# Diagonal matrices made earlier, C's products woven between part A's products, carried states by one more identity product

## The chip, the cores and the metric

One core of a Trainium2 chip runs the whole program. TensorE multiplies, VectorE (DVE) and ScalarE (ACT) work element by element, GpSimd (POOL) sets small tiles, and SyncE (SP) issues nearly all transfers. The metric is the device time of one execution in microseconds (us). The kernel before took 145.25 us, the median of three runs (145.24 to 145.46).

## The reference

The output has two halves side by side, of 2048 rows and 448 columns each.

Part A is a linear recurrence with complex diagonal state (448 states) over 2048 steps:

```python
Lam_bar = jnp.exp(dt * Lam)
B_bar = ((Lam_bar - 1.0) / Lam)[:, None] * Bmat
Bu = jnp.einsum("bld,pd->blp", x + 0j, B_bar)
for t in range(L):
    h = Lam_bar[None, :] * h + Bu[:, t, :]
y = 2.0 * jnp.einsum("blp,dp->bld", hseq, Cmat).real + x * Dskip[None, None, :]
```

Part B is attention with 16 heads of 28 columns, where each position sees itself and seven earlier ones, two steps apart:

```python
qkv = (x @ wqkv).reshape(B, S, 3, H, Dh)          # q, k, v
idx = pos[:, None] - (jnp.arange(8) * 2)[None, :] # positions looked at
logits = einsum("bhsd,bhswd->bhsw", q, k[idx]) * Dh ** -0.5   # -1e9 where idx < 0
o = einsum("bhsw,bhswd->bhsd", softmax(logits), v[idx])
out = o.reshape(B, S, D) @ wo
```

## The kernel before

**Part A.** A complex state is held as a pair of real ones, so the 448 states are seven tiles (m = 0 to 6) of 128 partitions, 64 real and 64 imaginary. Multiplying the states by a power of Lam_bar is a product on TensorE with a 128x128 matrix of four diagonal blocks. `mat` (L595) makes such a matrix for all seven m at once on VectorE, out of a pattern `Dm` and the powers in `Scat`. The powers are listed in `KPOW` (L44): index 0 to 5 are the powers 1, 2, 3, 4, 8 and 12, index 6 to 12 are 16 up to 1024; one more, "g", scales C. `mats_behind` (L590) makes several of them and puts each behind a given VectorE instruction.

The 2048 steps are split into 512 groups of four. Level 1 (`level1_halves` L653 for m = 0 to 3, `level1` L632 for the rest) computes the state inside each group, h[0] to h[3], each from the one before. `scan` (L665) sums four groups to one and then doubles over 128 columns in seven rounds, each a product with a power and a cast on ScalarE. It runs three times, for m = 0 to 3, 4 to 5 and 6. `ends` (L688) builds the states at the ends of all groups, G: three of every four columns by six products, the fourth by a copy on ScalarE (L693). `correct` (L706) adds to h[b] what came into the group, M[b+1] times G, in one of two ways: "A" adds h by an identity product and casts on ScalarE (two products), "V" has one product and an add on VectorE (L715). `y` (L722) makes an output tile from four products with the skip vector's diagonal `Dg` (made in `skip`, L580) and seven with C. C is loaded as rows (`load_c`), transposed by a transfer (`turn_c`, L501) and multiplied by "g" (`setup_c`, L609).

**Part B.** q, k and v are products of x with weights. VectorE multiplies q with shifted k (`products`, L298, each in a queue behind the one before, `queued` L293), and TensorE sums over a head's columns with 0/1 matrices (`sums`, L315). `softmax(hf)` (L344) has five steps: two transposes with maxima on VectorE, two products that subtract the maxima, followed by exponentials on ScalarE, and the sums `den` with the reciprocal `rec` on VectorE. `pv` (L400) multiplies the weights with shifted v and adds up, on VectorE, for eight w; after each w it runs what its list `between` has. The last rows that a shift needs come by `halo` copies (L235). `tail` (L422) transposes the sums by a transfer into oT and multiplies by wo.

**The order.** TensorE's order is written out by hand: every product is chained behind the one before (`chain`, L85). In `lanes` (L97) products of 64 rows run in two lanes, upper and lower half of the array, one step of the loop giving one product to each lane. `weave` is a list of (step, functions): when the loop reaches the step, the functions run and their products stand between those of the lanes. These are called visits here. Behind the lanes, scans, level 1, `ends` and wo's first products follow, and then a list `line` of corrections and y products, into which the products of the "V" corrections are put at fixed distances (L871 to L877). All other engines' instructions are put in an order before the run by a planner that starts what its own costs hold to be ready, in program order where several are. PSUM has eight banks: four with tag "mm", two "pt" and two "lg"; `ps` (L75) takes a bank by tag, and an instruction that writes a bank waits until its former content has been read. The lanes use "mm" and "pt" in turn, the softmaxes "lg".

Of the kernel before, what the change touches and what calls it, by code (L numbers as in the profile page):

```python
# [14 lines left out]
f32 = mybir.dt.float32  # L15
# [3 lines left out]
D = 448  # L19
T = 16  # L20
NCH = 128
KT = 4
KP = 112
KA = 128
NF = 512
# [9 lines left out]
NM = 7  # L35
# [3 lines left out]
PAD = 64  # L39
MH = ((0, 4), (4, 6), (6, 7))  # L40
# [3 lines left out]
KPOW = [1, 2, 3, 4, 8, 12] + [T << s_ for s_ in range(NST)]  # L44
NPW = len(KPOW)
# [401 lines left out]
class PartA:  # L447
# [132 lines left out]
    def skip(self):  # L580
        nc, ident = self.nc, self.cx.ident
        ptd = self.cx.ps([KA, KT], bf16, "pt_d", "lg")
        self.cx.chain(nc.tensor.transpose(ptd[:], self.drow[:], ident[0:KT, 0:KT]).ins)
        dsk = self.pool.tile([KA, KT], f32, name="dsk")
        nc.scalar.copy(dsk[:], ptd[:])
        self.Dg = self.pool.tile([KA, KT, KA], bf16, name="Dg")
        for k in range(KT):
            nc.scalar.activation(self.Dg[:, k, :], ident[:], ACT.Copy, scale=dsk[:, k:k + 1])

    def mats_behind(self, keys, after):  # L590
        for i in keys:
            key = "g" if i == "g" else KPOW[i]
            self.cx.order(self.mat(key, self.Scat[:, NPW if i == "g" else i]), after, "NoSync")
# [12 lines left out]
            self.mats[key] = t_[:].rearrange("p h q m -> p m (h q)")  # L606
        return self.nc.vector.tensor_tensor(t_[:], in0, in1, op=ALU.mult).ins  # L607

    def setup_c(self, eng):  # L609

        for m in range(NM):
            ps = self.cx.ps([NCH, D], f32, "c_ps", "pt")
            self.nc.tensor.matmul(ps[:], lhsT=self.mats["g"][:, m, :], rhs=self.cT[:, :, m, :], start=True, stop=True)
            self.cx.ev(eng, self.C[:, m, :], ps[:])

    def alloc_h(self):
        pool = self.pool
# [70 lines left out]
    def ends(self, mh):  # L688
        nc, cx = self.nc, self.cx
        M, v = self.mats, self.h[3]  # L690
        hc = self.pbuf[mh][NST % 2]
        gv = self.G[:, :, 1:1 + NF].rearrange("p m (c a) -> p m c a", a=4)
        nc.scalar.copy(gv[:, MH[mh][0]:MH[mh][1], :, 3], hc[:, :, PAD:PAD + NCH])  # L693
        for m in range(*MH[mh]):
            vm = v[:, m, :]
            hp = hc[:, m - MH[mh][0], PAD - 1:PAD - 1 + NCH]
            ps = cx.ps([NCH, 3 * NCH], f32, "gt", "mm")
            mm = [(cx.ident[:], vm[:, 0:3 * NCH], 0, 3), (M[4][:, m, :], vm[:, 0:2 * NCH], 1, 3),
                  (M[8][:, m, :], vm[:, 0:NCH], 2, 3), (M[4][:, m, :], hp, 0, 1), (M[8][:, m, :], hp, 1, 2),
                  (M[12][:, m, :], hp, 2, 3)]  # L700
            for i, (l_, r_, c0, c1) in enumerate(mm):
                nc.tensor.matmul(ps[:, c0 * NCH:c1 * NCH], lhsT=l_, rhs=r_, start=(i == 0), stop=(i == 5),  # L702
                                 skip_group_check=True)
            nc.scalar.copy(gv[:, m, :, 0:3], ps[:].rearrange("p (a c) -> p c a", a=3))

    def correct(self, b, m, eng):  # L706
        nc, cx, out = self.nc, self.cx, []
# [31 lines left out]
@with_exitstack  # L739
def body(ctx: ExitStack, tc: tile.TileContext, A_x, A_Lre, A_Lim, A_Bre, A_Bim, A_Cre, A_Cim, A_logdt, A_Dskip,  # L740
         B_x, B_wqkv, B_wo, out):
    nc = tc.nc
    pool = ctx.enter_context(tc.tile_pool(name="sb", bufs=1))
    psum = ctx.enter_context(tc.tile_pool(name="ps", bufs=1, space=bass.MemoryType.PSUM))
    out_v = out[0].rearrange("(p j) e -> p j e", j=T)
    cx = Ctx(tc, pool, psum)
    b = PartB(cx, B_x, B_wqkv, B_wo, out_v[:, :, D:2 * D])
    a = PartA(cx, A_x, A_Lre, A_Lim, A_Bre, A_Bim, A_Cre, A_Cim, A_logdt, A_Dskip, out[0].rearrange("(n b) e -> n b e", b=4)[:, :, 0:D])
    parts = ((512, 1024), (1024, 1536), (1536, 2048))
    b.alloc()  # L750
    b.load_xn(0, 2)
    a.load_params()
    b.load_w(D, 0, D, nc.scalar)
    b.load_xn(2, 4)
    cx.consts()
    a.consts()
    b.clear()
    nc.scalar.activation(cx.spot2[:], cx.wz[0:1, 0:1], ACT.Exp)
    b.load_w(0, D, D, nc.sync)
    for g in parts:  # L760
        b.load_x(*g)
    b.consts()
    b.load_w(2 * D, 2 * D, D, nc.sync)
    a.load_bc()
    a.load_d()
    a.load_x()
    a.turn_b()
    b.zero_halo(b.vd)
    b.load_wo()
    a.load_c()  # L770
    cx.warm(8)
    a.turn_params()
    turns = [lambda i=i: b.turn_x(i, "VAVV"[i], ("pt", "lg")[i // 2]) for i in range(4)]
    for f in turns[:2]:
        for ins in f():
            cx.chain(ins)
    a.params(b.turned["V"])
    cx.warm(2)

    def later():  # L780
        b.mix_w(a.reduced)
        return ()

    def first():
        b.products(0, 0)
        return ()

    def second():
        b.products(0, 0, (2,), (2,))
        return ()  # L790

    def third():
        b.products(0, 1, (0, 1))
        return ()

    values = [b.proj(j, "A") for j in (*range(HJ, T), 6, 7, 4, 5, 2, 3, 0, 1)]
    qk, soft = b.qk(), {}
    weave = [(5, turns[2:] + [later]), (BEGIN[0], [first]), (BEGIN[1], [second]), (BEGIN[2], [third])]
    weave += [(s_, [f]) for s_, f in zip(WEAVE, qk)]
    weave.sort(key=lambda x: x[0])  # L800

    def turn():
        a.mats_behind(["g"], b.product)
        soft[1] = b.softmax(1)
        return soft[1][0][0]() + soft[1][0][1]()

    def prepare():
        a.mats_behind([0, 3, 4], b.maxima)
        return soft[1][0][4]()

    def begin():
        b.halo(b.vd, 6, HALO)
        b.halo(b.vd, 0, 6)
        a.turn_c()
        a.skip()
        a.alloc_h()
        soft[0] = fs, at0 = b.softmax(0)

        def put(*fs):
            return lambda after: [x for f in fs for x in ((f() if callable(f) else a.mats_behind([f], after)) or ())]  # L820

        soft["pv"] = b.pv(1, soft[1][1], 0, 4, between=[put(*fs[:2]), put(5, 6), put(*fs[2:4]), put(7, 8), put(fs[4]), put(9, 10)])
        soft["put"] = put
        return more()

    def more():
        return next(soft["pv"]) + next(soft["pv"])

    weave += [(168, [turn])] + [(171 + 2 * i, [lambda i=i: soft[1][0][2 + i]()]) for i in range(2)] + [(177, [prepare])]
    weave += [(181, [begin]), (205, [more]), (215, [more])]  # L830
    cx.lanes([b.proj_t(t0, t1, g, "A") for t0, t1, gs in ((0, 256, (0, 1, 2, 4, 5, 6)), (256, 512, (0, 1, 2)), (0, 512, (3,)), (256, 512, (4, 5, 6)))
              for g in gs]
             + [b.proj_t(*t, g, "A") for t in parts for g in range(7)] + values
             + [a.level1_halves(b_, m) for b_ in range(4) for m in range(*MH[0])], weave, 20)
    at0, put, wo = soft[0][1], soft["put"], b.outs
    deque(soft["pv"], 0)
    deque(b.pv(1, soft[1][1], 4, 8, between=[put(11, 12), put(), put(1, 2)]), 0)
    a.alloc_scan()
    for mh in range(3):
        if mh:  # L840
            a.level1(mh)
        a.scan(mh)
        if mh == 0:
            a.setup_c("A")
    cx.order(wo[0]()[0][0], a.last, "NoSync")
    for mh in range(3):
        a.ends(mh)
    cx.ya = pool.tile([NCH, 8, D], bf16, name="ya", tag="cn")
    line, extra, steps = [], [], []
    todo = [(b_, m) for b_ in (1, 2) for m in range(NM)][2:]  # L850

    def each(ins):
        cx.vchain(ins)
        steps.append(ins)
        if len(steps) >= 7 and todo:
            extra.extend(a.correct(*todo.pop(0), "V"))

    def wo_line(lists):
        return [(i, 0.19) for l_ in lists for i in l_]

    for b_, m in [(0, m) for m in range(NM)] + [(1, 0), (1, 1)]:
        line += a.correct(b_, m, "A")
    line += wo_line(wo[1]())
    deque(b.pv(0, at0, 0, 4, each=each), 0)
    deque(b.pv(0, at0, 4, 8, True, each=each), 0)
    for b_, r in itertools.product((3, 0, 1, 2), range(4)):
        line += a.y(r, b_)
        if (b_, r) == (1, 3):
            line += wo_line(wo[2]())
    line += wo_line([wo[3](i) for i in range(2)])  # L870
    t, n = 0.0, 0  # L871
    for ins, dt in line:
        if n < len(extra) and t >= 1.55 * n:
            cx.chain(extra[n][0])
            t, n = t + extra[n][1], n + 1
        cx.chain(ins)
        t += dt  # L877
# [31 lines left out]
```

## Time and profile before

| | |
|---|---|
| median of three runs | 145.25 us |
| the profiled execution | 145.12 us |
| its span, first to last instruction | 143.2 us |
| TensorE busy | 137.2 us (96%) |
| VectorE busy | 123.2 us (86%) |
| ScalarE busy | 90.9 us (63%) |
| share of the last chain on TensorE / VectorE | 69% / 23% |

The span is the part of the execution from its first to its last instruction. A row of a timeline gives start, busy time, engine, line, operation, tile written and tiles read, and, in brackets, how long the engine was idle before it and what ended the wait. For TensorE the busy time of a row includes the pipeline's end, so the distance between two starts, not the row's own length, is what a product costs. The chain that ended last goes back from the last instruction to what released each; an engine can be on it that another would have held up anyway.

### The profile page before, as it was taken

Reading aid. Unit: us, or ns where it says so; the run is one execution under the profiler, and the core shown is the slowest. Engines: PE = TensorE matmul, PEld = TensorE weight load, DVE = VectorE, ACT = ScalarE, POOL = GpSimd, SP = SyncE. Lnnn points to the kernel's source line nnn. Section 1 sums busy time; section 2 is a strip of 40 time slices with the busy share of each in tenths; the row PEclk is TensorE's granted clock in tenths of the full one; section 3 lists DMA queues with packets and bytes.
Section 4 is the critical chain, followed back from the end, with each engine's and each line's share of the span. In section 5 each row is a group of like instructions: output and inputs, shape, how many; then the busy total and the mean of one; then the engine's idle time right before and its main releaser. Section 6 shows DMA issues by size and latency. Waiting matters only on the chain.

```text
span 143.2 us, 3302 instructions
## 1 busy us (share of the span) xinstructions
PE 137.2 (96%) x1260; PEld 78.0 (54%) x1260; DVE 123.2 (86%) x153; ACT 90.9 (63%) x200; POOL 10.5 (7%) x108
## 2 busy tenths in 40 slices
PE   6999999999999998999999999999999999999991
PEld 2466445444666654446665456668556555555540
DVE  4488764989999889999999999999999999999011
ACT  3476678667786766583589897889973222435440
POOL 7211100100000000000101000000000000000000
PEclk9999999999999999999999999999999999999999
DMA  4989899899964979990003800018102182211963
GB/s 114 293 171 143 199 209 158 149 197 159 169 122 96 184 112 278 247 195 0 0 0 64 69 0 0 0 30 198 36 32 98 64 174 89 95 64 64 136 221 128
DMA packets 45166, 17.03 MB, mean 119 GB/s; under 512 B 37267, under 2 KB 44769, under 8 KB 45151
## 3 DMA queue, kind: packets, MB, share of 16 engines
q1 hardware_dynamic: 44586, 16.36, 58.1%
q10 hardware_dynamic: 565, 0.46, 1.1%
q8 instruction: 10, 0.16, 0.5%
q14 instruction: 5, 0.04, 0.1%
HBM read 3.91 MB, written 3.67 MB: 53 GB/s over the span
## 4 chain that ended last, share of the span: by engine, by line
PE 69%; DVE 23%; ACT 3%; issue 2%; POOL 0%; DVEq 0%; ACTq 0%; POOLq 0%
PE qk_ps L130 16%; PE y_ps L731 15%; DVE pvb L414 8%; PE wo_ps L437 7%; DVE pvb L417 6%; PE v_ps L130 5%; PE lg L323 5%; PE l L638 5%; PE co L711 3%; PE warm L73 3%; DVE pr L312 2%; DVE mat L607 2%; PE y_ps L727 2%; PE gt L702 2%; PE l L683 2%
## 5 line engine op out<-in xcount | busy, mean ns | idle before, releaser
L414 DVE TENSOR_TENSOR pvb<-attn,vd 128x1792 bf16<-128x1792 bf16 (+1 forms) x33 | 34.3, 1063 | 0.0
L417 DVE TENSOR_TENSOR pvb<-pvb 128x1792 bf16<-128x1792 bf16 (+1 forms) x29 | 30.8, 1061 | 0.3
L130 PE MATMUL qk_ps<-xbT,wqkv_nat 64*128 64x512 bf16 (+1 forms) x210 | 24.0, 335 | 0.4 <-POOL spot L139 0.3
L312 DVE TENSOR_TENSOR pr<-q,kd 128x3072 bf16<-128x3072 bf16 x11 | 19.0, 1754 | 3.8 <-ACT q L156 3.4
L734 ACT CAST ya<-y_ps 128x448 bf16<-128x448 f32 x16 | 8.5, 532 | 17.2 <-PE y_ps L731 16.1
L731 PE MATMUL y_ps<-Ccat,h 128*128 128x448 bf16 x84 | 17.9, 353 | 0.0
L130 PEld LDWEIGHTS <-wqkv_nat 64*128 64x128 bf16 x210 | 11.0, 94 | 10.7 <-POOL spot L139 3.1
L130 PE MATMUL l1h<-xaT,Bcat 64*128 64x512 bf16 x112 | 15.4, 377 | 0.0
L437 PE MATMUL wo_ps<-wo_p,oT 128*128 128x448 bf16 x64 | 13.9, 352 | 0.0
L638 PE MATMUL l<-xaT,Bcat 128*128 128x512 bf16 x48 | 13.6, 379 | 0.0
L156 ACT CAST kd<-qk_ps 128x512 bf16<-128x512 f32 (+4 forms) x26 | 10.4, 423 | 4.5 <-PE qk_ps L130 4.3
L130 PE MATMUL v_ps<-wqkv_nat,xbT 64*128 64x448 bf16 x112 | 13.1, 360 | 0.0
L156 ACT CAST q<-qk_ps 128x512 bf16<-128x512 f32 (+2 forms) x23 | 9.9, 456 | 2.0 <-PE qk_ps L130 1.8
L731 PEld LDWEIGHTS <-h 128*128 128x128 bf16 x84 | 7.5, 98 | 5.6
L139 POOL MEMSET spot<- 1x1 f32 x63 | 5.6, 89 | 59.5 <-PE qk_ps L130 25.6
L156 ACT CAST vd<-v_ps 128x448 bf16<-128x448 f32 x16 | 7.6, 528 | 3.7 <-PE v_ps L130 3.5
L130 PEld LDWEIGHTS <-Bcat 64*128 64x128 bf16 x112 | 7.0, 94 | 5.3 <-issue 0.4
L312 DVE TENSOR_TENSOR kd<-q,kd 128x3072 bf16<-128x3072 bf16 x5 | 8.8, 1755 | 1.2 <-ACT q L156 1.2
L686 ACT CAST pbuf<-l 128x512 bf16<-128x512 f32 (+2 forms) x21 | 8.7, 416 | 1.4 <-PE l L683 1.2
L130 PEld LDWEIGHTS <-xbT 64*128 64x128 bf16 x112 | 7.3, 145 | 4.1 <-issue 1.3
L437 PEld LDWEIGHTS <-oT 128*128 128x128 bf16 x64 | 6.0, 98 | 5.5 <-issue 0.6
L649 ACT CAST h<-l1h 128x512 bf16<-128x512 f32 x12 | 6.3, 602 | 3.5 <-PE l1h L130 3.5
(133 smaller groups left out, 218.9 us busy)
## 6 DMA issues: line engine op xcount, KB each, us to landing
out_dram<-ya SPq DMA_DIRECT2D x20, 112.0 KB, 1.7
out_dram<-yb SPq DMA_DIRECT2D x12, 112.0 KB, 3.0
vd<-vd SPq DMA_DIRECT2D x1, 784.0 KB, 5.6
wqkv_nat<-in_B_wqkv_dram SPq DMA_DIRECT2D x2, 336.0 KB
vd<-vd SPq DMA_DIRECT2D x1, 588.0 KB
xn<-in_B_x_dram SPq DMA_DIRECT2D x2, 224.0 KB, 3.8
cn<-in_A_C_re_dram SPq DMA_DIRECT2D x4, 98.0 KB, 3.1
cn<-in_A_C_im_dram SPq DMA_DIRECT2D x4, 98.0 KB, 3.2
```

The costliest lines, as they stand in the source:

```text
L130: ins = mm(g["ps"], lhsT=l_, rhs=r_, start=first, stop=not (g["left"][0] or g["left"][1]), skip_group_check=True).ins
L156: return self.nc.scalar.copy(out, in_).ins
L312: self.queued(V.tensor_tensor(pr, q[0][:, qu].unsqueeze(2).to_broadcast([KA, KT - 1, 4, n]), self.shifted(self.kT[:, 2 * i + qu], s), op=A ...
L323: out.append(mm(lg[32 * t:32 * t + 32, n * qu:n * qu + n], lhsT=l_, rhs=r_, start=not (s or qu or c), stop=(s == 1 and c == KT - 1), skip_ ...
L414: each(V.tensor_tensor(t_[:, c0:c1], at[:, w, jl0 + c0:jl0 + c1, :].unsqueeze(2).to_broadcast([NCH, c1 - c0, DH, H]), self.vd[:, off + c0: ...
L417: ins = V.tensor_tensor(acc[:, c0:c1], acc[:, c0:c1], t_[:, c0:c1], op=ALU.add).ins
L437: done.append(nc.tensor.matmul(ps[:], lhsT=oT[:, 7 * i + 3 * odd + k, :], rhs=self.wo_p[:, odd, k, :], start=(k == 0), stop=(k == KT - 1)) ...
L638: nc.tensor.matmul(ps[:], lhsT=self.Bcat[:, m, k, :], rhs=self.xT[:, b, k, :], start=(k == 0), stop=(b == 0 and k == KT - 1))
L649: self.nc.scalar.copy(h, ps)
L686: nc.scalar.copy(dst[:, :, PAD:], ps[:])
L731: out.append(nc.tensor.matmul(ps[:], lhsT=self.state(m, r, b), rhs=self.C[:, m, :], start=False, stop=(m == NM - 1), skip_group_check=True ...
L734: nc.scalar.copy(ya, ps[:])
```

## The change

Five edits, all in the order and form of the work:

- The matrices M[1], M[4], "g" and M[8] are made among the first products of q and k (`early`, queued with them). In their former places come others: three in `turn`, three in `prepare`, and the list `between` of the first pv is left without mats.
- C's seven products become visits in the lanes at steps 218, 222, 226 and 242, with banks of tag "lg" instead of "pt". `turn_c` moves ahead of the halo copies in `begin`, and the skip vector's diagonal moves from `begin` to step 242.
- The two later visits of the first pv, with the steps of softmax 0, move from steps 205 and 215 to 199 and 211.
- The fourth column of G comes from a seventh product in `ends`, with the identity, and one cast of 512 columns; the copy goes.
- Corrections: five instead of nine of kind "A", sixteen instead of twelve of kind "V", which start behind the ninth VectorE instruction of the last pv pair instead of the seventh.

```diff
     def skip(self):
...
-        self.cx.chain(nc.tensor.transpose(ptd[:], self.drow[:], ident[0:KT, 0:KT]).ins)
+        out = [nc.tensor.transpose(ptd[:], self.drow[:], ident[0:KT, 0:KT]).ins]
...
+        return out
...
-    def setup_c(self, eng):
-
-        for m in range(NM):
-            ps = self.cx.ps([NCH, D], f32, "c_ps", "pt")
-            self.nc.tensor.matmul(ps[:], lhsT=self.mats["g"][:, m, :], rhs=self.cT[:, :, m, :], start=True, stop=True)
-            self.cx.ev(eng, self.C[:, m, :], ps[:])
+    def setup_c(self, *ms):
+
+        out = []
+        for m in ms:
+            ps = self.cx.ps([NCH, D], f32, "c_ps", "lg")
+            out.append(self.nc.tensor.matmul(ps[:], lhsT=self.mats["g"][:, m, :], rhs=self.cT[:, :, m, :], start=True, stop=True).ins)
+            self.cx.ev("A", self.C[:, m, :], ps[:])
+        return out
...
-        gv = self.G[:, :, 1:1 + NF].rearrange("p m (c a) -> p m c a", a=4)
-        nc.scalar.copy(gv[:, MH[mh][0]:MH[mh][1], :, 3], hc[:, :, PAD:PAD + NCH])
...
-            ps = cx.ps([NCH, 3 * NCH], f32, "gt", "mm")
+            ps = cx.ps([NCH, NF], f32, "gt", "mm")
...
-                  (M[12][:, m, :], hp, 2, 3)]
+                  (M[12][:, m, :], hp, 2, 3), (cx.ident[:], hc[:, m - MH[mh][0], PAD:PAD + NCH], 3, 4)]
...
-            nc.scalar.copy(gv[:, m, :, 0:3], ps[:].rearrange("p (a c) -> p c a", a=3))
+            nc.scalar.copy(self.G[:, m, 1:1 + NF].rearrange("p (c a) -> p c a", a=4),
+                           ps[:].rearrange("p (a c) -> p c a", a=4))
...
+    def early(*keys):
+        for k in keys:
+            ins = a.mat("g" if k == "g" else KPOW[k], a.Scat[:, NPW if k == "g" else k])
+            if b.product is not None:
+                cx.order(ins, b.product, "NoSync")
+            b.product = ins
+
     def first():
+        early(0)
         b.products(0, 0)
         return ()
 
     def second():
         b.products(0, 0, (2,), (2,))
+        early(3)
         return ()
 
     def third():
         b.products(0, 1, (0, 1))
+        early("g", 4)
         return ()
...
     def turn():
-        a.mats_behind(["g"], b.product)
+        a.mats_behind([5, 6, 7], b.product)
...
     def prepare():
-        a.mats_behind([0, 3, 4], b.maxima)
+        a.mats_behind([8, 9, 10], b.maxima)
...
     def begin():
+        a.turn_c()
         b.halo(b.vd, 6, HALO)
         b.halo(b.vd, 0, 6)
-        a.turn_c()
-        a.skip()
         a.alloc_h()
...
-        soft["pv"] = b.pv(1, soft[1][1], 0, 4, between=[put(*fs[:2]), put(5, 6), put(*fs[2:4]), put(7, 8), put(fs[4]), put(9, 10)])
+        soft["pv"] = b.pv(1, soft[1][1], 0, 4, between=[put(*fs[:2]), put(), put(*fs[2:4]), put(), put(fs[4])])
...
-    weave += [(181, [begin]), (205, [more]), (215, [more])]
+    weave += [(181, [begin]), (199, [more]), (211, [more])]
+    weave += [(218 + 4 * m, [lambda m=m: a.setup_c(m, m + 1)]) for m in (0, 2, 4)] + [(242, [lambda: a.setup_c(6), a.skip])]
...
-        if mh == 0:
-            a.setup_c("A")
...
-    todo = [(b_, m) for b_ in (1, 2) for m in range(NM)][2:]
+    todo = [(b_, m) for b_ in range(3) for m in range(NM)][5:]
...
-        if len(steps) >= 7 and todo:
+        if len(steps) >= 9 and todo:
...
-    for b_, m in [(0, m) for m in range(NM)] + [(1, 0), (1, 1)]:
-        line += a.correct(b_, m, "A")
+    for m in range(5):
+        line += a.correct(0, m, "A")
```

More of the change, by code (lines that the diff above doesn't have):

```diff
@@ L696, in ends @@
             hp = hc[:, m - MH[mh][0], PAD - 1:PAD - 1 + NCH]
-            ps = cx.ps([NCH, 3 * NCH], f32, "gt", "mm")
+            ps = cx.ps([NCH, NF], f32, "gt", "mm")
             mm = [(cx.ident[:], vm[:, 0:3 * NCH], 0, 3), (M[4][:, m, :], vm[:, 0:2 * NCH], 1, 3),
                   (M[8][:, m, :], vm[:, 0:NCH], 2, 3), (M[4][:, m, :], hp, 0, 1), (M[8][:, m, :], hp, 1, 2),
-                  (M[12][:, m, :], hp, 2, 3)]
+                  (M[12][:, m, :], hp, 2, 3), (cx.ident[:], hc[:, m - MH[mh][0], PAD:PAD + NCH], 3, 4)]
             for i, (l_, r_, c0, c1) in enumerate(mm):
-                nc.tensor.matmul(ps[:, c0 * NCH:c1 * NCH], lhsT=l_, rhs=r_, start=(i == 0), stop=(i == 5),
+                nc.tensor.matmul(ps[:, c0 * NCH:c1 * NCH], lhsT=l_, rhs=r_, start=(i == 0), stop=(i == 6),
                                  skip_group_check=True)
-            nc.scalar.copy(gv[:, m, :, 0:3], ps[:].rearrange("p (a c) -> p c a", a=3))
+            nc.scalar.copy(self.G[:, m, 1:1 + NF].rearrange("p (c a) -> p c a", a=4),
+                           ps[:].rearrange("p (a c) -> p c a", a=4))
     def correct(self, b, m, eng):
```

## The prediction

> **What bounds the kernel now.** I read the page's busy shares first, then the chain that ended last, then the timelines of TensorE, VectorE and SyncE between 45 and 100 us. Busy shares:
>
> ```profile
> PE 137.2 (96%) x1260; PEld 78.0 (54%) x1260; DVE 123.2 (86%) x153; ACT 90.9 (63%) x200; POOL 10.5 (7%) x108
> ```
>
> TensorE is idle for 6.0 us of 143.2: 1.25 before its first product, 3.2 behind its last, 1.5 in all between. So a change pays by taking products off TensorE, and costs whatever makes TensorE wait. The chain confirms it from 99.9 us on, with TensorE alone down to the last cast:
>
> ```profile
> 1.25 3.59 PE warm L73 x8
> ...
> 100.13 0.21 PE co L710
> 100.34 0.22 PE co L711
> ...
> 140.02 0.62 DVE ya L158
> ```
>
> The first row matters below: eight products of 512 columns took 3.59 us, 0.449 each, where a 512-column product takes 0.2155 later (the spacing of the "co" rows). TensorE started from idle at half rate (the page's line of granted clock does not show it; the durations do), and the two "warm" products of 5.93 us still took 0.405 each, so that lasted till about 6.7, some 5.4 us.
>
> VectorE's timeline has three holes early on, in the column of idle time before a row:
>
> ```profile
> 11.23 3.43 DVE L312 TENSOR_TENSOR pr<-q,kd 128x3072 bf16<-128x3072 bf16 x2 [0.78 <-ACT q L156]
> 16.79 1.76 DVE L312 TENSOR_TENSOR kd<-q,kd 128x3072 bf16<-128x3072 bf16 x1 [0.83 <-ACT q L156]
> 23.30 1.76 DVE L312 TENSOR_TENSOR pr<-q,kd 128x3072 bf16<-128x3072 bf16 x1 [2.59 <-ACT q L156]
> ```
>
> The most telling pair is one product on TensorE and its reader on VectorE:
>
> ```profile
> 63.64 0.62 PE L370 MATMUL den<-e,ident 128*128 128x128 bf16 x8
> 72.79 0.96 DVE L373 RECIPROCAL rec<-den 128x128 bf16<-128x128 f32 x1
> ```
>
> The sums of the second softmax (den) are finished at 64.2, but VectorE, whose order is fixed before the run, reads them 8.6 us later, behind the add of w=6. In program order the reciprocal stands behind the add of w=5. So the planner that wrote the order did not expect den at three picks (w=6 product, w=7 product, add of w=6), which start 14.6 to 16.6 us behind the first pv product of 55.16: it takes the 64-row products to be slower than they are. From den of softmax 1 (visit at step 177) to this one (step 215) lie 38 steps of the loop at L106, real spacing 0.2155 us; to miss those picks it must reckon with about 0.45 each, both halves in a row instead of side by side. Nobody in this kernel suffers: den's bank (tag "lg", two banks) is next wanted by wo_ps, after 91 us.
>
> The transpose for C, and the skip vector's cost:
>
> ```profile
> 57.82 5.12 SPq L505 DMA_TRANSPOSE Ccat<-cn  x1
> 55.17 0.41 PE L355 MATMUL lt<-ident,lgs 128*128 128x128 bf16 x4 [0.38 <-ACT dsk L585]
> ```
>
> **The change, part by part.** Durations are of the profiled execution: 145.12 us, 143.2 of it the span; the median of the runs, 145.25, is 0.13 more.
>
> Early mats. One mat costs VectorE 0.60 us (spacing of the L607 rows), g 1.75. M[1] goes in the hole of 0.78, M[4] in that of 0.83, g and M[8], 2.35, in that of 2.59. Slack 0.18, 0.23, 0.24, so 0; behind them queue the q-k products, and if a hole shrank by its slack, the sums on TensorE would come some 0.2 later. In turn(), three mats (1.80) take g's place (1.75), in prepare() three take the place of three: 0. Six mats, 3.6 us, leave the pv sequence, four of them (2.4) ahead of the reciprocal. VectorE is not what ends the kernel: its last add ends at 132.56, TensorE's y products at 136.83.
>
> Identity products. Nine corrections with a product more become five: 4 x 0.2155 = -0.86 on TensorE. VectorE takes four adds more, 4 x 0.60 = 2.4, covered by the 3.6 that left, as is the later start of its adds (behind nine pv operations instead of seven, 2.0). Uncovered, its end would come 2.4 later; the last transpose of oT behind it landed at 137.2 and is wanted at 138.4, so 1.2 would show.
>
> Carried states. Seven identity products of 128 columns, 0.055 each (row L673): +0.38 on TensorE. ScalarE loses three copies (L693: 1.36, 0.78, 0.49) and its L704 casts grow from 384 to 512 columns, 0.50 to about 0.59 (row L686). ScalarE has room: 0.
>
> The skip vector leaves the visit at step 181. There the second half of lt waited for its bank (row above); the next step began at 55.50 and now does at about 54.75: -0.75. At step 242 it costs 0.06 and part of a visit.
>
> The visit for the exponentials moves from step 205 to 199. TensorE would be there at 58.9, but VectorE's second maximum ends at 59.45: +0.4. The denominator's visit, step 215 to 211, then runs at 62.4 to 62.95 and step 218 comes at 64.5.
>
> C's products as visits. Seven products of 0.187 move from the scan to the lanes: 0 net, since the scan's steps keep level 1's products as cover (57 of 0.2155, 12.3 us; the first scan took 10.0 from its first cast at 73.39 to its last). Each visit costs beyond its products 0.11 us (den: 0.55 for eight of 0.055), so four cost +0.44. The wait of 0.21 for a mat at 81.17 goes: -0.21.
>
> SyncE. Programmed first in begin(), the transpose now needs the C loads (landed 55.3) and the last v product (54.2); the halo copies queue behind it if it goes out first. It landed 8.4 us after issue, at 66.26. If the halos still go first, C's first product waits for that landing; if it goes first, it lands by 63.8, and the halo rows for w=5 land at about 65.8 instead of 59.0, 1.4 late for VectorE.
>
> The wait for den's bank. C's first two products at step 218 take both "lg" banks, and one is den's, free only when the reciprocal has read it. VectorE's order decides. Without the mats, from 55.16: two products, maximum, add, maximum bring it to 59.37, then one pv operation per 1.0 us. The planner expected den between 16.6 and 17.6 us into the sequence (the last pick that missed it and the one that took it); four steps of 0.45 and some 0.3 for the skip vector less, that is 14.5 to 15.5. VectorE's picks now lie at 14.2, 15.2 and 16.2, so the reciprocal follows eleven pv operations, or one more or less: it starts at 70.4 (69.4 to 71.4) and ends at 71.35. TensorE runs in order and stands from 64.5, but for one short product, to 71.35. Before, step 218 came at 64.84: +6.51. The bounds for this wait are 0 (reciprocal done by 64.5) and 9.3 (reciprocal unmoved at 72.79, done 73.75).
>
> The clock behind the wait. No row shows TensorE idle for over 0.4 us after the start. Bounds: 0, as with those short gaps, and 2.7, half of those 5.4 us. The nearest row for a start from several idle us is the first: the eight products lost 3.59 - 8 x 0.2155 = 1.87, and I take that. [...]
>
> Sum: +6.51, then -0.19 (C's first product is done ahead of the wait), -0.86, +0.38, +0.06, +0.44, -0.21: +6.13. With the clock +1.87: +8.0. 145.25 + 8.0 = 153.3.
>
> **The rivals.** (a) The wait with the clock at full: 145.25 + 6.1 = 151.4; for it, C's first product may break the idle stretch in two; against it, half rate at the start.
> (b) No wait, the other side: the planner puts the reciprocal at most four pv operations behind the second maximum, so that it is read by 64.5. Then -0.75 + 0.4 - 0.86 + 0.38 + 0.06 + 0.44 - 0.21 = -0.54: 144.7, 144.2 to 145.0 as the 0.4 and the visits vary. The price is small, as TensorE only loses four products and a stall. Against it: the reciprocal's place in the profile, missed by 8.6 us.
> (c) The reciprocal is early enough, but the transpose still goes out behind the halos: wait to 66.3, +1.8 - 0.54: 146.5.
> (d) A small wait eats the gain: within 0.2%.
>
> **How the numbers follow.** The three runs lie 0.22 us apart, so under 0.2%, 0.29 us, is no change that can be told. Chances: forecast 0.44 (151.9 to 155.3: reciprocal one operation earlier or later, halo late by 1.4, clock loss to 2.7); (a) 0.30 (150.4 to 152.9); (c) 0.07; (b) 0.15; (d) 0.04. Faster 0.15, within 0.04, slower 0.81. The forecast, (a) and (c) hold 0.81; as the order is inferred, I let the range reach into (b): 144.6 to 155.3.
>
> **What would show it.** In the changed profile: L373 of softmax 0 some ten to twelve pv operations behind the second maximum and near 70.4; an idle of 5 to 7 us before C's second product on TensorE, released by that L373; behind it products of 512 columns well over 0.2155 apart, or a smaller digit in the line of granted clock; three shrunk holes on VectorE before 23.30; five identity rows of co; VectorE waiting for co near 100 us, as TensorE is late; lt back to back at 54.2. The prediction is wrong if the reciprocal is read by 64.5, or if C's products find other banks free.

## The result and the profile after

| | before | after |
|---|---|---|
| median of four runs | 145.30 us (145.24 to 145.46) | 153.56 us (153.26 to 154.45) |
| profiled execution | 145.12 us | 153.78 us |
| its span | 143.2 us | 151.7 us |
| TensorE busy | 137.2 us (96%) | 138.7 us (91%) |
| mean granted clock | 1.0 | 0.976 |

The ratio is 1.0577 [1.0531, 1.0624]: slower by 5.8%, 8.3 us, and 0.3 us above the forecast of 153.3. The page of the changed kernel, busy times and two rows of the 40 slices:

```profile
span 151.7 us, 3303 instructions
PE 138.7 (91%) x1263; PEld 76.7 (51%) x1263; DVE 125.4 (83%) x157; ACT 88.4 (58%) x193; POOL 10.5 (7%) x108
PE   6899999999999999902997999999999999999991
PEclk9999999999999999996599999999999999999999
```

A slice is 3.8 us. Slices 18 and 19 (64.5 to 72.1) show TensorE nearly idle, and slices 19 and 20 a clock of 0.6 and 0.5. TensorE's timeline names who held it:

```profile
63.89 0.59 PE L130 MATMUL l1h<-xaT,Bcat 64*128 64x512 bf16 x3
65.40 0.36 PE L615 MATMUL c_ps<-Ccat,matg 128*128 128x448 bf16 x1 [0.92 <-DMA Ccat<-cn]
71.08 0.53 PE L615 MATMUL c_ps<-Ccat,matg 128*128 128x448 bf16 x1 [5.32 <-DVE rec L373]
83.41 0.22 PE L676 MATMUL l<-h,ident 128*128 128x128 bf16 x1 [1.09 <-ACT h L654]
```

C's first product waits 0.92 us for the transpose of C, its second 5.32 us for the reciprocal `rec`, because both "lg" banks are then taken and one still holds den. (The four visits stand at steps 218, 226, 234 and 242: `218 + 4 * m` for m = 0, 2 and 4 gives the first three, not 218, 222 and 226 as the list of the change has it.) VectorE's timeline has that reciprocal, and a wait of ten microseconds near the end:

```profile
58.45 0.68 DVE L357 TENSOR_REDUCE mx<-lt 128x64 bf16<-128x512 f32 x1
...
69.07 1.08 DVE L417 TENSOR_TENSOR pvb<-pvb 128x1792 bf16<-128x1792 bf16 x1
70.07 0.95 DVE L373 RECIPROCAL rec<-den 128x128 bf16<-128x128 f32 x1
...
109.57 0.69 DVE L717 TENSOR_TENSOR h<-co,h 128x512 bf16<-128x512 f32 x1 [10.05 <-PE co L713]
```

Between the second maximum (58.45) and the reciprocal stand eleven pv operations. The last row is the sign of a TensorE that is late: VectorE has nothing left but the corrections. The busy time by stretch (length, then busy time and instructions of TensorE, its weight loads, VectorE, ScalarE and GpSimd, then the granted clock, the DMA share and GB/s) shows the clock:

```profile
64.40:69.30 4.90, 0.44 (x3) 0.11 (x2) 4.90 (x6) 0.53 (x1) 0.08 (x1) 1.00 0.00 0
69.40:71.00 1.60, 0.00 (x0) 0.00 (x0) 1.60 (x3) 0.00 (x0) 0.00 (x0) 0.50 0.00 0
71.10:76.10 5.00, 5.00 (x21) 1.36 (x22) 5.00 (x6) 1.89 (x4) 0.18 (x2) 0.50 0.49 92
76.30:82.00 5.70, 5.70 (x49) 2.93 (x45) 5.70 (x8) 3.79 (x10) 1.44 (x11) 1.00 0.00 0
```

From 69.36 to 76.19 the clock is 0.50. TensorE works from 71.08 on, with 21 products in 5.0 us where 49 fit into 5.7 us later.

The two traces stage by stage (TensorE's starts; the changed kernel's trace begins 0.32 us earlier, its first reciprocal being at 53.05 instead of 53.37):

| stretch | before | after | difference | forecast |
|---|---|---|---|---|
| step 218: its lane product / C's second product | 64.84 | 71.08 | +6.24, with the 0.32 +6.56 | +6.51 |
| from there to the first scan product | 6.79 (to 71.63) | 12.33 (to 83.41) | +5.54 | +3.49 |
| to the first "co" product | 28.11 (to 99.74) | 25.68 (to 109.09) | -2.43 | -1.14 |
| to TensorE's end | 40.24 (to 139.98) | 39.46 (to 148.55) | -0.78 | -0.86 |

The differences come to +8.89, less the 0.32 to +8.57, which is also that of TensorE's end. The forecasts in the last column are the prediction's terms sorted by stretch, +8.0 in all: in the second row six of C's products (1.12), the visits' 0.44, the skip vector's 0.06 and the clock's 1.87; in the third -1.31 for C's products, -0.21 for the mat's wait and +0.38 for the identity products. In the second row 2.05 us more came than forecast: 0.69 by the clock, 1.09 by the wait for ScalarE in the last row of TensorE's timeline above, and 0.27 that no row names. In the third row 1.29 us less came.

### The profile page after: what moved, and what is told of

It is laid out like the page before. It is cut to its first block, busy times and chain, and to the rows that moved or that the text cites. A ratio compares the mean times of both kernels' runs of the same rounds, so it can differ in the third digit from the quotient of the medians.

```text
span 151.7 us, 3303 instructions
## 1 busy us (share of the span) xinstructions
PE 138.7 (91%) x1263; PEld 76.7 (51%) x1263; DVE 125.4 (83%) x157; ACT 88.4 (58%) x193; POOL 10.5 (7%) x108
## 4 chain that ended last, share of the span: by engine, by line
PE 74%; DVE 15%; ACT 3%; DMA 2%; issue 2%; SPq 1%; POOL 0%; DVEq 0%; POOLq 0%
PE qk_ps L130 15%; PE y_ps L733 14%; PE wo_ps L437 8%; PE l L641 7%; PE l1h L130 5%; DVE pvb L414 5%; PE v_ps L130 5%; PE lg L323 4%; DVE pvb L417 4%; PE co L713 3%; PE l L686 3%; DVE pr L312 2%; PE y_ps L729 2%; DMA prow<-in_A_Lambda_im_dram 2%; PE gt L703 2%
## 5 line engine op out<-in xcount | busy, mean ns | idle before, releaser
L717 DVE TENSOR_TENSOR h<-co,h 128x512 bf16<-128x512 f32 x16 | 11.0, 686 | 10.2 <-PE co L713 10.0
L733 PE MATMUL y_ps<-Ccat,h 128*128 128x448 bf16 x84 | 18.7, 353 | 0.0
L130 PE MATMUL l1h<-xaT,Bcat 64*128 64x512 bf16 x112 | 18.0, 406 | 0.0
L641 PE MATMUL l<-xaT,Bcat 128*128 128x512 bf16 x48 | 12.9, 379 | 0.0
```

The lines of the kernel that those rows point to most:

```text
L130: ins = mm(g["ps"], lhsT=l_, rhs=r_, start=first, stop=not (g["left"][0] or g["left"][1]), skip_group_check=True).ins
L641: nc.tensor.matmul(ps[:], lhsT=self.Bcat[:, m, k, :], rhs=self.xT[:, b, k, :], start=(k == 0), stop=(b == 0 and k == KT - 1))
L717: cx.vchain(nc.vector.tensor_tensor(h, ps[:], h, op=ALU.add).ins)
L733: out.append(nc.tensor.matmul(ps[:], lhsT=self.state(m, r, b), rhs=self.C[:, m, :], start=False, stop=(m == NM - 1), skip_group_check=True ...
```

## The experiments

Theory: the 8 us are TensorE's wait for den's bank, so the place of the reciprocal in VectorE's order, and the half clock that the wait brings on. Rivals: the wait costs no clock; the cost is that of the visits themselves or of the other edits, and stays when the reciprocal is early. The first four below ran on one chip, the next four on a second, the last two on a third, each beside the kernel before (145.35, 145.38 and 145.17 us).

**1. Keep TensorE busy in the wait.** Base: the changed kernel. Thirty products of zeros are written to C's first bank ahead of C's first product, which overwrites it; nobody reads them.

```diff
         for m in ms:
             ps = self.cx.ps([NCH, D], f32, "c_ps", "lg")
+            for _ in range(30 if m == 0 else 0):
+                out.append(self.nc.tensor.matmul(ps[:], lhsT=self.cx.wz[:, 0:NCH], rhs=self.cx.wz[:, 0:D], start=True, stop=True).ins)
```

> The changed kernel with 30 products of zeros, 448 columns each, put into C's first bank ahead of C's first product, about 5.7 us of work that nobody reads. The wait for the reciprocal stays: C's second product still starts near 71.1. My theory (the wait costs twice: 5.3 us of standing still, and half rate for some 5.4 us behind it, 2.6 us lost): the clock stays full and the time falls by 2.6 to about 150.9. Rival (the slow products behind the wait have another cause, such as banks or ScalarE behind the visits): no change, 153.5.

Measured: 151.54 us (150.91 to 151.61), ratio 1.0424 [1.0381, 1.0466]. TensorE's timeline, and below it the stretch behind the wait:

```profile
64.03 5.85 PE L616 MATMUL c_ps<-wz 128*128 128x448 bf16 x30
69.72 0.35 PE L617 MATMUL c_ps<-Ccat,matg 128*128 128x448 bf16 x1
70.70 0.35 PE L617 MATMUL c_ps<-Ccat,matg 128*128 128x448 bf16 x1 [0.63 <-DVE rec L373]
```

```profile
71.00:76.20 5.20, 5.20 (x43) 2.36 (x44) 5.20 (x7) 4.03 (x9) 0.29 (x4) 1.00 0.47 88
```

C's second product starts where it did (its trace begins 0.38 earlier), the clock stays at 1.00, and 43 products run in 5.2 us where 21 ran in 5.0. From that product to the scan it takes 9.97 us (70.70 to 80.67) instead of 12.33. So the lost clock is worth 2.36 us by the traces, 2.0 by the medians, and the wait itself does not go away.

**2. The reciprocal early.** Base: the changed kernel. Den's visit is put ahead of w=4, and pv's operations from w=4 on are ordered behind the reciprocal; the diff leaves out where it is remembered.

```diff
+                if self.gate is not None:
+                    cx.order(ins, self.gate, "NoSync")
...
-        soft["pv"] = b.pv(1, soft[1][1], 0, 4, between=[put(*fs[:2]), put(), put(*fs[2:4]), put(), put(fs[4])])
+        soft["pv"] = b.pv(1, soft[1][1], 0, 4, between=[put(*fs[:2]), put(), put(*fs[2:4])])
...
+    def sums():
+        out = soft[0][0][4]()
+        b.gate = b.rec
+        return out + more()
```

> The changed kernel with the reciprocal of softmax 0 ahead of the pv operations from w=4 on, in VectorE's order; nothing is taken out. My theory (den's bank, held until VectorE reads it, is the whole wait): the reciprocal runs at 63.1 to 64.0, C's second product follows the first, which still waits for its transpose until 65.4; 5.3 us of waiting and 2.6 us of half rate go: 145.6. Rival (the visits themselves, the transpose or ScalarE hold TensorE up): 150 or more.

Measured: 146.24 us (145.16 to 146.96), ratio 1.0058 [1.0026, 1.0091], 0.6 above what was expected. VectorE's reciprocal, and TensorE's timeline:

```profile
63.04 0.95 DVE L373 RECIPROCAL rec<-den 128x128 bf16<-128x128 f32 x1
```

```profile
64.88 0.55 PE L620 MATMUL c_ps<-Ccat,matg 128*128 128x448 bf16 x2 [0.54 <-DMA Ccat<-cn]
75.05 0.22 PE L681 MATMUL l<-h,ident 128*128 128x128 bf16 x1 [1.09 <-ACT h L659]
```

The reciprocal starts at 63.04, C's two products run back to back and the clock never falls. One instruction's place in VectorE's order was 7.3 us of the 8.3. What is left over the kernel before is in two waits, for the transpose (0.54) and for ScalarE at the scan (1.09).

**3. The reciprocal half-way.** Base: the changed kernel. The same ordering, but of pv's operations from the product of w=6 on only, to see how short an idle stretch still costs the clock.

```diff
+    b.gate = b.rec
```

> The changed kernel with the reciprocal of softmax 0 ahead of the pv operations from w=6 on: three pv operations earlier than in the changed kernel, so C's second product should start at 68.1 and TensorE stand still for 2.3 us in place of 5.3. If the clock falls only behind a longer idle time: 153.6 - 3.0 - 2.6 = 147.9. If it falls behind 2.3 us as well: 150.5.

Measured: 150.91 us (149.73 to 151.44), ratio 1.0379 [1.0312, 1.0445]. TensorE's timeline, and the stretches:

```profile
64.85 0.36 PE L620 MATMUL c_ps<-Ccat,matg 128*128 128x448 bf16 x1
68.42 0.53 PE L620 MATMUL c_ps<-Ccat,matg 128*128 128x448 bf16 x1 [3.21 <-DVE rec L373]
```

```profile
64.10:65.20 1.10, 0.96 (x7) 0.23 (x4) 1.10 (x2) 0.42 (x1) 0.18 (x2) 1.00 0.00 0
65.30:67.50 2.20, 0.00 (x0) 0.00 (x0) 2.17 (x4) 0.48 (x1) 0.00 (x0) 1.00 0.00 0
67.50:68.40 0.90, 0.00 (x0) 0.00 (x0) 0.90 (x3) 0.00 (x0) 0.00 (x0) 0.51 0.00 0
68.40:74.30 5.90, 5.88 (x25) 1.70 (x26) 5.90 (x7) 2.48 (x5) 0.18 (x2) 0.50 0.00 0
```

The expectation for a falling clock holds. C's first product found the transpose landed, so the idle stretch was 3.2 us and not the 2.3 it was sized for. The clock fell at 67.52, 2.3 us behind the last product, and stayed at half for 6.8 us. The last section sets this beside the other runs.

**4. C's products back behind the first scan, the other edits kept.** Base: the changed kernel.

```diff
-            ps = self.cx.ps([NCH, D], f32, "c_ps", "lg")
+            ps = self.cx.ps([NCH, D], f32, "c_ps", "pt")
...
-    weave += [(218 + 4 * m, [lambda m=m: a.setup_c(m, m + 1)]) for m in (0, 2, 4)] + [(242, [lambda: a.setup_c(6), a.skip])]
+    weave += [(242, [a.skip])]
...
+        if mh == 0:
+            a.setup_c(*range(NM))
```

> The changed kernel with C's products back behind the first scan and in banks of tag pt, as before; the skip vector stays at step 242, all other edits stay. My theory (the visits carry the whole loss, the other edits gain): no wait on TensorE between 64 and 71 and a time below the kernel before, 144.3 by my terms (143.5 to 144.8). Rival (the loss lies in the moved softmax steps or corrections): 150 or more.

Measured: 145.20 us (144.66 to 145.59), ratio 0.9987 [0.9967, 1.0008]. The whole loss is the visits', as expected; but the other edits did not give the 1 us that was expected of them. TensorE's timeline has a wait at the scan, and ScalarE's shows what stands ahead of it:

```profile
72.59 0.22 PE L676 MATMUL l<-h,ident 128*128 128x128 bf16 x1 [0.95 <-ACT h L654]
```

```profile
70.31 1.28 ACT L588 ACTIVATE Dg<-ident,dsk 128x128 bf16<-128x128 bf16 x4
71.50 2.02 ACT L654 CAST h<-l1h 128x512 bf16<-128x512 f32 x4
```

The skip vector at step 242 puts four scalings for `Dg`, 1.28 us, on ScalarE ahead of the last four casts of h, and the scan reads these. This is the miss of 0.9.

**5. The changed kernel with each wait mended.** Experiment 2, with the transpose ahead of the second pair of halo copies, the skip vector at step 234, C's last product listed at 230 and the exponentials' visit at 201.

```diff
-    weave += [(181, [begin]), (199, [more]), (211, [more])]
-    weave += [(218 + 4 * m, [lambda m=m: a.setup_c(m, m + 1)]) for m in (0, 2, 4)] + [(242, [lambda: a.setup_c(6), a.skip])]
+    weave += [(181, [begin]), (201, [more]), (211, [sums])]
+    weave += [(218 + 4 * m, [lambda m=m: a.setup_c(m, m + 1)]) for m in (0, 2, 4)] + [(230, [lambda: a.setup_c(6)]), (234, [a.skip])]
```

> The reciprocal-first kernel (e2_rec_first) with three more edits against the waits that its trace still shows: C's transpose goes out ahead of the second pair of halo copies (wait of 0.54 for it), the skip vector moves from step 242 to 234 and C's last product from 242 to 230 (wait of 1.09 for ScalarE before the first scan), the visit for the exponentials from 199 to 201 (wait of 0.24). Theory (each of these waits is on TensorE's path in full): 146.2 - 1.9 = 144.3, below the kernel before. Rival (VectorE is by then the bound, its last sums come no earlier and wo's last products wait): no gain over 145.4.

Measured: 144.35 us (143.65 to 144.66), ratio 0.9929 [0.9901, 0.9957]. All five edits of the change are in it, some at other steps, and it is 0.7% faster than the kernel before. TensorE's two waits that are left:

```profile
69.06 0.55 PE L622 MATMUL c_ps<-Ccat,matg 128*128 128x448 bf16 x2
70.05 0.35 PE L622 MATMUL c_ps<-Ccat,matg 128*128 128x448 bf16 x1 [0.43 <-ACT Ccat L156]
...
74.93 0.22 PE L683 MATMUL l<-h,ident 128*128 128x128 bf16 x1 [0.30 <-ACT h L661]
```

C's last product did not run at step 230. The loop works the list `weave` off in the order of its entries, and the entry of step 230 stands behind that of 234; so it ran at 234, as third product in a row for two banks (69.06 twice, then 70.05), and the wait of 0.43 is made by that.

**6. Experiment 4 with the skip vector eight steps earlier.**

```diff
-    weave += [(242, [a.skip])]
+    weave += [(234, [a.skip])]
```

> The kernel without visits for C (e4_no_visits) with the skip vector at step 234 in place of 242 and nothing else. Theory (the four scalings of the skip vector, 1.28 us on ScalarE, stand ahead of the last casts of level 1, and the first scan waits 0.95 for them): 145.2 - 0.95 = 144.3. Rival (the scan waits for its casts wherever the scalings stand, and the moved edits gain nothing): 145.2.

Measured: 144.15 us (143.59 to 144.58), ratio 0.9917 [0.9885, 0.9949]. The scan now starts without a wait:

```profile
71.59 0.23 PE L676 MATMUL l<-h,ident 128*128 128x128 bf16 x1
```

So four instructions on ScalarE, 1.28 us together, cost TensorE about 1 us at one place and nothing eight steps earlier.

**7. The visits alone.** Base: the kernel before; only `setup_c`, its banks and its place are changed.

```diff
+    weave += [(218 + 4 * m, [lambda m=m: a.setup_c(m, m + 1)]) for m in (0, 2, 4)] + [(242, [lambda: a.setup_c(6)])]
...
-        if mh == 0:
-            a.setup_c("A")
```

> The kernel before with C's products as visits at the same four steps and in banks of tag lg, and nothing else of the change: mats, softmax steps, corrections, skip vector and the order of transfers as before. Theory (visits plus VectorE's order make the wait): the reciprocal runs at 72.8 as before, C's second product starts at 73.8, TensorE stands some 7 to 9 us and then runs at half rate, and the time is 156.0 (154.5 to 157), more than with the whole change. Rival (the moved mats or softmax steps are needed for the wait): under 148.

Measured: 156.30 us (two runs, 156.29 and 156.31), ratio 1.0754 [1.0702, 1.0805]. TensorE's timeline, and VectorE's reciprocal:

```profile
66.56 0.36 PE L614 MATMUL c_ps<-Ccat,matg 128*128 128x448 bf16 x1 [1.57 <-DMA Ccat<-cn]
73.72 0.53 PE L614 MATMUL c_ps<-Ccat,matg 128*128 128x448 bf16 x1 [6.80 <-DVE rec L373]
```

```profile
72.72 0.95 DVE L373 RECIPROCAL rec<-den 128x128 bf16<-128x128 f32 x1
```

The reciprocal is where it always was (72.72), and now somebody waits for it. The change's own reordering had made this wait 1.5 us shorter; the visits made it.

**8. The mats alone.** Base: the kernel before; only the places of the mats are changed (`early`, and the lists of three).

```diff
-        a.mats_behind(["g"], b.product)
+        a.mats_behind([5, 6, 7], b.product)
...
-        a.mats_behind([0, 3, 4], b.maxima)
+        a.mats_behind([8, 9, 10], b.maxima)
```

> The kernel before with the mats moved as in the change and nothing else. Theory (VectorE's 3.6 us are off the path; only the wait of 0.21 for a mat in the first scan goes): 145.1 to 145.4, no change that can be told. Rival (VectorE's lead reaches the end): 144 or less. Rival (the mats in the three holes delay the q-k products): 145.8 or more.

Measured: 145.00 us (144.37 to 145.31), ratio 0.9965 [0.9945, 0.9984]. From the first scan product to the first "co" it takes 27.80 us (71.81 to 99.61) instead of 28.11: the wait of 0.21 at 81 us for a mat is gone, as forecast, and this is most of what this edit gives.

**9. The visits tuned further.** Experiment 5, with the skip vector at step 214 and C's last product listed at 232, to take the two waits left there.

```diff
+    weave += [(181, [begin]), (201, [more]), (211, [sums]), (214, [a.skip])]
+    weave += [(218 + 4 * m, [lambda m=m: a.setup_c(m, m + 1)]) for m in (0, 2, 4)] + [(232, [lambda: a.setup_c(6)])]
```

> The repaired kernel (e5_repaired) with the skip vector at step 214 and C's last product at 232, against the two waits left in its trace, 0.43 for a bank of C and 0.30 for ScalarE's casts behind the scalings. Theory (both on the path): 144.35 - 0.7 = 143.65. Rival (ScalarE's scalings now delay C's casts and with them the next visit): 144.3 or more.

Measured: 144.07 us (143.78 to 144.26 in five runs, 145.95 in the sixth), ratio 0.9905 [0.9875, 0.9935]. The expected 143.65 was missed: the two waits stayed, 0.43 at C's last product and 0.28 in the scan. Neither edit touched what makes its wait. C's last product again stands behind the entry of step 234 and ran with it (68.84, 69.04 and 69.83). And the scan's wait is not the scalings': they ran at 64.03, and ScalarE was idle ahead of the last four casts of h, which the scan waits for:

```profile
72.26 2.15 ACT L661 CAST h<-l1h 128x512 bf16<-128x512 f32 x4 [1.51 <-PE l1h L130]
```

**10. No visits, tuned.** Experiment 6 with the exponentials' visit at step 201.

```diff
-    weave += [(181, [begin]), (199, [more]), (211, [more])]
+    weave += [(181, [begin]), (201, [more]), (211, [more])]
```

> The kernel without visits and with the skip vector at 234 (e6_no_visits_skip234), with the visit for the exponentials at step 201 in place of 199. Theory (the wait of 0.24 for the second maximum is on the path): 144.15 - 0.24 = 143.9. Together with e9 this tells whether C's products as visits are worth anything once no wait is left: by stage, the scan stretch is 2.4 shorter without them and the lanes longer by 1.31 of products and 0.44 of visits, so e9 should be some 0.3 to 0.6 below e10. Rival (the visits gain nothing): e9 not below e10.

Measured: 143.87 us (143.74 to 144.37 in five runs, 146.03 in the sixth), ratio 0.9892 [0.9860, 0.9925]: the lowest median, but not to be told from experiments 6 and 9. With and without visits the same time comes about in two ways. The lanes take 2.56 us longer with them (53.50 to 73.50, against 54.23 to 71.67 without), the stretch from the first scan product to the first "co" 2.21 us less (25.79 against 28.00). ScalarE's timeline at the end of the first scan tells why it is more than C's products, 1.31; "pbuf" rows are the scan's casts, "h" rows level 1's. Without visits:

```profile
82.26 0.58 ACT L689 CAST pbuf<-l 128x512 bf16<-128x512 f32 x1
83.07 0.58 ACT L652 CAST h<-l 128x512 bf16<-128x512 f32 x1 [0.22 <-PE l L645]
84.15 0.58 ACT L654 CAST h<-l 128x512 bf16<-128x512 f32 x1 [0.49 <-PE l L645]
85.23 0.58 ACT L654 CAST h<-l 128x512 bf16<-128x512 f32 x1 [0.49 <-PE l L645]
86.31 0.37 ACT L681 CAST pbuf<-l 128x256 bf16<-128x256 f32 x1 [0.49 <-PE l L679]
```

With visits (experiment 9):

```profile
84.03 0.59 ACT L696 CAST pbuf<-l 128x512 bf16<-128x512 f32 x1
84.86 0.59 ACT L661 CAST h<-l 128x512 bf16<-128x512 f32 x1 [0.24 <-PE l L652]
85.94 0.37 ACT L688 CAST pbuf<-l 128x256 bf16<-128x256 f32 x1 [0.49 <-PE l L686]
```

The first scan's casts take equally long in both, 8.9 us from first to last (73.34 to 82.26, 75.16 to 84.03). But where the scan holds C's products and their seven casts, five steps of level 1 fit under it, and where it doesn't, seven; so three steps are left behind it instead of one, at 1.08 us a step: 2.14 of the 2.21 us lie between the two "pbuf" rows shown (4.05 against 1.91). ScalarE is the reason: it is busy for 9.7 of the scan's first 10 us in experiment 10 and for 8.0 in experiment 9. The longer lanes give it all back: 1.31 us of products, the wait of 0.43 for a bank, and 0.82 for the visits themselves and what no row names. As the 0.43 comes from the order of a list, no run shows visits without a wait, and whether these would gain stays open.

## Why the prediction was right

Forecast and result agree to 0.3 us. That the range held the time says little, since 144.6 to 155.3 holds all four rivals as well; what tells the forecast from them is the wait, the clock and the signs named for them. And 0.3 us is closer than the terms deserve: two were off by over 1 us, with opposite signs, and that they cancelled is luck. By its steps:

- **The wait for den's bank** (+6.51). Measured +6.56. The reciprocal was forecast at 70.4 behind eleven pv operations and came at 70.07, with the 0.32 at 70.39, behind eleven. TensorE was forecast at step 218 at 64.5 and had its last row ahead of it done at 64.48, with the 0.32 at 64.80. Experiments 2 and 7 show that it is this wait: mended, 7.3 us go; with the visits alone, it is longer. The inference that carried it, the planner's reckoning of den by the place of an instruction that nobody waited for, held; the planner's costs themselves no run shows. Experiment 8 bears it out a second time: with the old steps and no mats in the pv sequence the reciprocal follows thirteen pv operations, 17.2 us behind the first, in the stretch of 16.6 to 17.6 that the prediction had inferred.
- **The clock** (+1.87, bounds 0 and 2.7). It fell, so rival (a), 151.4, is out; experiment 1, which is (a) made real, took 151.54. The term was too small: 2.0 to 2.4 us by experiment 1, and 2.56 by the trace (half of the 5.11 us from 71.08 to 76.19). Behind the stall the clock stood at 0.50 from 69.36 on, and it was full again 5.1 us after work had begun again, at 76.19. That is near the 5.4 us behind the upper bound of 2.7, where the 1.87 counted the first eight products (3.59 us) alone.
- **ScalarE has room: 0.** This step was wrong, twice, with opposite signs. It was said of the carried states; of the skip vector only TensorE's 0.06 was counted, and its four scalings on ScalarE, 1.28 us, were not. In the changed kernel the scan waited 1.09 for ScalarE; 0.3 of it stays when the scalings stand elsewhere (experiments 5 and 9), so they cost about 0.8, and 0.95 where C stands in the scan (experiments 4 and 6). In the scan, on the other hand, ScalarE had no room as long as C's casts were there: the stretch came 1.29 us shorter than forecast (-2.43 for -1.14). Experiments 9 and 10 account for 0.9 of it (2.21 less C's 1.31), the identity products below for 0.3. That the move of C's products would be "0 net" was therefore right for another reason than the one given: they cost 1.31, the visits' own time and the waits in the lanes, and gave back 2.2 us in the scan, where two more of level 1's steps took their place. The two errors, +1.09 and -1.29, cancelled to 0.2 us; either alone would have put the forecast a microsecond off.
- **Exponentials earlier** (+0.4). The visit took 0.93 us instead of 0.54, with an idle of 0.23 for the second maximum: +0.39. Two steps later (experiment 10) the idle is gone.
- **The skip vector out of step 181** (-0.75). From the first l1h product to the one behind the lt transposes took 0.96 us instead of 1.63: -0.67.
- **Identity products** (-0.86 for four fewer in the corrections; +0.38 for seven in `ends`). From the first "co" to the end -0.78; experiment 4, which has C in the scan as before, took 28.00 from first scan product to first "co" instead of 28.11, where +0.38 and -0.21 had been put: some 0.3 better than forecast.
- **Early mats** (0) and the mat's wait (-0.21). The holes on VectorE shrank to 0.22 and 0.32 us, the first to nothing. Experiment 8 gave -0.35% [-0.55%, -0.16%], at the edge of what was expected.
- **SyncE.** The question left open, whether the transpose or the halos go first, came out between: three of the four halo copies went ahead, then the transpose at 56.12, which landed 9.2 us later, at 65.3. C's first product waited 0.92 us for it, in the shade of the longer wait; alone it is worth 0.54 (experiment 2), rival (c) at a third of its 1.8.

Rival (b), 144.7 without the wait, comes nearest to experiment 5, 144.35, where the other waits are mended too. In the change as it stands it failed by the reciprocal's place; with the reciprocal early and nothing else (experiment 2, 146.24) the transpose's 0.54 and the scan's 1.09 are still there, so that rival (c), 146.5, met the time by other terms than its own.

## What to carry to other kernels

When a product is moved into banks that another engine has still to empty, look up the place of that reader in its own engine's order, not the moment its data is ready: an instruction that was 8.6 us late for no one became a stall of 5.3 us in the change and of 6.8 with the visits alone, with the clock at 0.50 behind it in both, once TensorE, whose products are chained in order, needed its bank. Before an operation is called free, count what it issues on every engine and look at what is queued behind it there; the four scalings cost 1 us at one step and nothing eight steps earlier. Moving work from one stage to another need not gain: here the scan became 2.2 us shorter and the lanes 2.6 us longer, and the fastest run without visits, 1.1% below the kernel before, has the other edits alone. And look in the trace whether an edit did what it says: the product listed at steps 230 and 232 never moved there.

## What the runs showed of the hardware

The trace has the times at which the granted clock changes. In the changed kernel it goes to full at 4.51 us, to half at 69.36, to full at 76.19 and to half at 151.28. The distances are 64.85, 6.83 and 75.09 us: 19, 2 and 22 times 3.413 us. In the kernel before (6.56 and 143.10) the distance is 40 times that. Around its wait, the clock is at half from 67.52 to 74.34 us in experiment 3 and from 67.75 to 77.99 in experiment 7, 6.82 and 10.24 us, so 2 and 3 times that. Six distances that are whole multiples of 3.413 us are what was measured; what makes the clock change, no run shows. These are stretches of 3.413 us counted from the changes around the waits, with what TensorE was busy in each (experiment 1, whose clock does not change there, has any such stretch that holds its wait of 0.63 us):

| run | stretch, us | TensorE busy, us | clock in it | at its end |
|---|---|---|---|---|
| changed kernel | 62.53 to 65.95 | 2.31 | full | stays |
| | 65.95 to 69.36 | 0.00 | full | falls |
| | 69.36 to 72.77 | 1.69 | half | stays |
| | 72.77 to 76.19 | 3.42 | half | returns |
| experiment 3 | 64.10 to 67.52 | 0.97 | full | falls |
| | 67.52 to 70.93 | 2.50 | half | stays |
| | 70.93 to 74.34 | 3.41 | half | returns |
| experiment 7 | 64.34 to 67.75 | 1.01 | full | falls |
| | 67.75 to 71.17 | 0.00 | half | stays |
| | 71.17 to 74.58 | 0.86 | half | stays |
| | 74.58 to 77.99 | 3.41 | half | returns |
| experiment 1 | with the wait of 0.63 | 2.78 | full | stays |

In these rows the clock fell at the end of stretches that were busy for 0.00, 0.97 and 1.01 us, and stayed full behind those with 2.31 and 2.78; it returned at the end of stretches that were busy throughout, and stayed at half behind those with 0.00, 0.86, 1.69 and 2.50. Values in between no run shows. The time from the last product to the fall was not the same in the three runs: the clock fell 3.6 us behind the last product in the changed kernel (the row of 65.40 ends at 65.76), 2.3 us behind it in experiment 3 and 0.8 us behind C's first product in experiment 7. Half rate went on for 5.1, 5.9 and 4.3 us after work had begun again, so the shortest of the three waits, that of experiment 3, lost the most to the clock.

Nor did the same kernel lose the same in each of its runs. In experiment 3 two runs had a mean clock of 0.977 (151.44 and 151.32 us) and two of 0.988 and 0.989 (149.73 and 150.50); 0.012 of 148 us is 1.8 us of lost clock, so by this estimate about 3.5 us at half, where the profiled run, the 151.44, had 6.8 (67.52 to 74.34). One of four runs of the changed kernel, the 154.45, had 0.966 instead of 0.976, by the same estimate about 3 us more at half. For the runs that were not profiled no trace shows when their clock changed.
